# Power-of-two scales made by ScalarE, and the first row roots on ScalarE, in a fused H3 convolution and SiLU feed-forward kernel

## The chip, the cores and the metric

The kernel runs on one core of a Trainium2 chip. The metric is device time in microseconds of one execution; the median of three runs of the kernel before is 1259.5 us. The core's engines work side by side, each with its own queue of instructions in a fixed order: TensorE (PE, matmuls into PSUM banks), VectorE (DVE, elementwise), ScalarE (ACT, activations with a per-partition scale and bias, and an optional sum over the row), GpSimd (POOL) and SyncE (SP), which here issue DMAs. They meet by semaphores only.

## The reference

For x = A_q (2048 rows of 1024), with a layer norm over the columns:

```python
xn = _layernorm(x, axis=-1)                     # (x - mean) / sqrt(var + 1e-5)
# _A_ref: q = xn
k_shift = sum over t of k_pad[:, t:t + S, :] * shift_k[:, ks - 1 - t]
kv = k_shift * v
y = irfft2(rfft2(kv padded) * rfft2(ssm_k padded))[:S] + kv * ssm_D
a = xn * y
# _B_ref
b = silu(xn @ w1) @ w2                          # w1 1024 x 3584, w2 3584 x 1024
out = x + a + b
```

## The kernel before, in words

All large products run on TensorE in float16. Each float32 operand is split into a high half (ScalarE, `split` at L369: copy times a scale) and a low half (VectorE, the difference), and each product is three matmuls: high by high, high by low, low by high (L887 to L889 for the first layer, L1016 to L1018 for the second, L1462 to L1464 and L1653 to L1655 for the convolution's transforms). For the halves to keep their bits, every operand is first brought to a fitting size by a **power of two** taken from its own energy. These scales are what the change is about.

Stages. In the first 80 us the 16 row tiles of x are loaded and normalized (`ln_rows`, L479), the first eight are transposed on TensorE (`turned`, L540) and split, and the first w1 columns are squared, scaled and split (`scales_w1`, L662, `factors_w1`). The first two column pairs of w1 are used plainly (`plain_unit`), over the four upper row tiles and then over the four lower ones; the others go through seven products instead of eight (Strassen's scheme, `units`, with `evacuate` emptying the banks on ScalarE and VectorE). The second layer does the same with the plain part first (`steps2`, `units2`). From about 190 us on the long convolution (`convolution`, from L1291) is woven between those matmuls, in eight groups of 128 channels: gate and short convolution (`gate`), split, forward transform on TensorE and VectorE, product in the frequency domain, `result_scales`, inverse transform, and the gating with xn (`gated`), whose results GpSimd adds to the output in HBM.

The order of all instructions is made before the program runs. Every piece of work is an `Op` with an engine, an estimated duration and the tiles that it reads and writes; generators yield Ops, and the planner `Order.run` (L176) takes at each step the Op that could start first by its own estimates, minus the generator's bias. So a changed Op in one place can move any later instruction of the program. The planner also adds 1.28 us where an Op needs another ScalarE table than the last one (L192).

The lines that the change touches:

- `norm` (L438): a matmul with ones (L448) sums squares over the partitions into PSUM. One VectorE Op, `chain` (L451), then reduces (L454), takes the maximum with 1e-30 and cuts the number to a power of two by two shifts of its bits (`pow2`, L434 and L435), and calls `then`.
- `then` in `scales_w1` (L680 to L682): two products with constants and a reciprocal, for the five scales of a column pair. In `gate` (L1384): a reciprocal and two products, for the signal and filter scales. In `result_scales` (L1564): four instructions, the last two multiplying by scales of the signal.
- `ln_rows`: statistics of each row tile (L497, L499), then for a group of row tiles (2, 2, 4 and 8 tiles) a chain of eleven VectorE instructions (L506 to L516): the inverse root by a first guess from the bits and two corrections. Then the rows are normalized, tiles 4 to 7 by ScalarE (L526), the others by VectorE (L528).
- `a_act` (L354): an activation; only Silu was marked as needing a table.
- The first activation (L1725) loads ScalarE's table, that of Silu, which also serves all the copies and squares.

Of the kernel before, what the change touches and what calls it, by code (L numbers as in the profile page):

```python
# [43 lines left out]
LB = 0.15  # L44
ON_ACT = (4, 5)
APPLY = (4, 5, 6, 7)
GUESS = 0x5f3759df

PRODUCTS = {"P1": ("A11", "B11"), "P7": ("S3", "T3"), "P6": ("S2", "T2"), "P2": ("A12", "B21"),
# [67 lines left out]
class Order:  # L117
# [4 lines left out]
    def __init__(self):  # L122
        self.free = defaultdict(float)
        self.wrote, self.read = {}, {}
        self.slots, self.patterns = {}, {}
        self.streams = []
        self.pipe = self.now = 0.0
        self.table = AF.Silu

    def cells(self, a):  # L130

# [168 lines left out]
def h3_ffn_kernel(ctx, tc, x, kp, vs, fs, shift, dskip, w1, w2, cfwd, cinv, out):  # L300
# [29 lines left out]
    def T(f, o, ins, us, m=0.1):  # L330
        return Op("PE", us, 0.3, f, ins, [o], m)
# [22 lines left out]
    def a_act(o, i, func, scale=1.0, bias=None, total=None):  # L354
        def f():
            kw = {} if bias is None else {"bias": bias}
            if total is not None:
                kw["accum_out"] = total
            nc.scalar.activation(o, i, func, scale=scale, **kw)  # L359
        ins = [i] + [s for s in (scale, bias) if s is not None and not isinstance(s, float)]  # L360
        p = A(f, o, ins)
        p.table = func if func == AF.Silu else None
        p.busy += 0.07 * (len(ins) - 1) - 0.06 * (i.space == bass.MemoryType.PSUM)
        if total is not None:
            p.busy += 0.19
            p.writes.append(total)
        return p
# [26 lines left out]
    for n, e in enumerate((14 - 64, 10 - 64, 8 - 64, 64 - 23, 64)):  # L394
        nc.vector.memset(powers[:, n:n + 1], 2.0 ** e)
    invc = cst.tile([P, 1], F32, name="invc")
    one = cst.tile([P, 1], F32, name="one")
    nc.vector.memset(one, 1.0)
    ones = one.to_broadcast([P, P])
# [38 lines left out]
    def norm(ring, ss, ns, then, flags, margin=1.5):  # L438

        yield ring.ready  # L440
        pt, tok = ring.tile([P, W])
        yield pw.ready
        e, etok = pw.tile([P, 2])

        cols, n = len(ns), sum(ns)

        def mm():
            nc.tensor.matmul(pt[:, 0:n], ones, ss, start=True, stop=True)  # L448

        def chain():  # L450
            for c, m in enumerate(ns):  # L451
                q = sum(ns[:c])
                if m > 1:
                    nc.vector.tensor_reduce(e[:, c:c + 1], pt[:, q:q + m], axis=AX.X, op=ADD)  # L454
                else:
                    nc.vector.tensor_copy(e[:, c:c + 1], pt[:, q:q + 1])
            pow2(e[:, 0:cols], e[:, 0:cols])
            then(e[:, 0:cols])

        yield T(mm, pt[:, 0:n], [ss], 0.25, m=margin)  # L460
        p = V(chain, e, [pt[:, 0:n]], us=1.1)
        p.writes = p.writes + flags[0]
        yield p
        tok.set()
        etok.set()
        for t in flags[1]:
            t.set()


# [9 lines left out]
    def ln_rows():  # L479
        for t0, n, bias in ((0, 2, 0.26), (2, 2, 0.17), (4, 4, LB), (8, 8, 0.03)):  # L480
            yield bias
            ag = lnp.tile([P, 8, 2], F32, name="ag", bufs=2)
            nt = lnp.tile([P, 3, 8], F32, name="nt", bufs=2)
            order_in = (8, 9, 12, 13, 10, 11, 14, 15) if n == 8 else range(t0, t0 + n)
            for t in order_in:
                yield flag["xt", t]
                xt = xts[t][0]
                if t in ON_ACT:
                    k = t - t0
                    yield a_act(wide, xt, AF.Copy, total=nt[:, 0, k:k + 1])  # L490
                    yield a_act(ag[:, k, 0:1], nt[:, 0, k:k + 1], AF.Copy, 1.0 / D)
                    yield a_act(wide, xt, AF.Square, -1.0, ag[:, k, 0:1], total=nt[:, 0, k:k + 1])
                    yield a_act(ag[:, k, 1:2], nt[:, 0, k:k + 1], AF.Copy, 1.0 / D)
                    continue
                st = lnp.tile([P, 2, 6], F32, name="st", bufs=2)
                for a in range(2):
                    yield V(lambda: nc.vector.bn_stats(st[:, a, :], xt[:, a * W:(a + 1) * W]), st[:, a, :],  # L497
                            [xt[:, a * W:(a + 1) * W]], us=0.65)
                yield V(lambda: nc.vector.bn_aggr(ag[:, t - t0], st), ag[:, t - t0], [st], us=0.2)  # L499
            q = slice(t0, t0 + n)  # L500
            mean, var, r = ag[:, 0:n, 0], ag[:, 0:n, 1], rstd[:, q]
            e, f, v = (nt[:, k, 0:n] for k in range(3))

            def chain():
                tt, ts, stt = nc.vector.tensor_tensor, nc.vector.tensor_scalar, nc.vector.scalar_tensor_tensor
                ts(v, var, EPS, None, op0=ADD)  # L506
# [9 lines left out]
                stt(r, e, 1.5, r, op0=ADD, op1=MUL)  # L516
            p = V(chain, r, [ag[:, 0:n]], us=1.8)
            p.writes += [e, f, v]
            yield p
            for k, t in enumerate(order_in):  # L520
                xt = xts[t][0]
                if k == (0 if t in APPLY else 1):
                    yield V(lambda: nc.vector.scalar_tensor_tensor(nmr[:, q], mean, -1.0, r, op0=MUL, op1=MUL), nmr[:, q], [ag[:, 0:n], r], us=0.2)
# [4 lines left out]
                yield V(lambda: nc.vector.tensor_scalar(xt, xt, ag[:, t - t0, 0:1], rstd[:, t:t + 1], op0=SUB, op1=MUL),  # L528
                        xt, [xt, ag[:, t - t0], rstd[:, t:t + 1]], us=0.78)
                flag["xn", t].set()  # L530
# [131 lines left out]
    def scales_w1():  # L662
        for n, (_, i) in enumerate(pairs):
            yield (0.25, 0.16, 0.1, 0.05)[min(n, 3)]
            m = 4 if n < 2 else 2
            if n >= NP:
                for a in range(m):
                    yield flag["raw", n, a]
                flag["scaled", n].set()
                continue  # L670
            yield sq_r.ready
            ss, tok = sq_r.tile([P, 4])
            for a in range(m):
                yield flag["raw", n, a]
                r = raws[n][2][a]
                yield a_act(junk[:, 0:r.shape[1]], r, AF.Square, total=ss[:, a:a + 1])

            def then(e, i=i):
                sc = wsc[:, i]
                nc.vector.tensor_scalar(sc[:, 3:5], powers[:, 3:5], e, None, op0=MUL)  # L680
                nc.vector.reciprocal(e, e)
                nc.vector.tensor_scalar(sc[:, 0:3], powers[:, 0:3], e, None, op0=MUL)  # L682
            yield from norm(ctxs["nm"], ss[:, 0:m], (m,), then, ([wsc[:, i]], [flag["scaled", n], tok]))

    spills = []

# [604 lines left out]
    def convolution(floor):  # L1291
# [57 lines left out]
        def gate():  # L1349

            for g in range(NG):
# [32 lines left out]
                def then(e):  # L1384
                    nc.vector.reciprocal(sc[:, 0:2], e)
                    nc.vector.tensor_scalar(sc[:, 0:2], sc[:, 0:2], 2.0 ** (15 - 64), None, op0=MUL)
                    nc.vector.tensor_scalar(sc[:, 2:4], e, 2.0 ** 64, None, op0=MUL)
                yield from norm(py_r, ss[:, 0:6], (4, 2), then, ([sc[:, 0:4]], [flag["scales", g]]), 4.0)

        CB = 0.03  # L1390

# [167 lines left out]
        def result_scales(g):  # L1559
# [1 line left out]
            yield flag["energy", g]  # L1561
            sc, ss = scs[g][0], sss[g][0]

            def then(e):  # L1564
                nc.vector.reciprocal(sc[:, 4:5], e)
                nc.vector.tensor_scalar(sc[:, 4:5], sc[:, 4:5], 2.0 ** (15 - 64 - 50), None, op0=MUL)
                nc.vector.scalar_tensor_tensor(sc[:, 5:6], e, 2.0 ** (64 - 41), sc[:, 2:3], op0=MUL, op1=MUL)
                nc.vector.tensor_tensor(sc[:, 5:6], sc[:, 5:6], sc[:, 3:4], op=MUL)
            yield from norm(py_r, ss[:, 8:12], (4,), then, ([sc[:, 4:6]], [flag["un", g], sss[g][1]]), 3.0)

        def inverse(g):

# [149 lines left out]
        yield from load_factors()  # L1722

    warm = lnp.tile([P, 1], F32, name="warm")
    nc.scalar.activation(warm, ones[:, 0:1], AF.Silu)  # L1725
    add(begin(), 0.05)
    add(warm_up(), 0.0)
    add(x_rows(), 0.13)
# [53 lines left out]
```

## Time and profile before

| | us |
|---|---|
| median of three runs (1259.02 to 1259.97) | 1259.5 |
| the profiled execution | 1259.29 |
| its span, first to last instruction | 1257.5 |
| TensorE busy | 1234.0 |
| VectorE busy | 1137.8 |
| ScalarE busy | 724.8 |
| GpSimd busy | 132.8 |

The profile is one execution. A row of a timeline has the start and the duration in us, the engine, the line, the operation, the tile written and the tile read, the shapes and a count; in brackets, how long the engine was idle before it and what ended that. A row of groups has the line, the engine, the operation and the count, then the busy time in us and the mean of one in ns, then the idle time before. Matmuls are pipelined: a 512-column one lasts 0.38 us in its row, but they start 0.21 to 0.22 us apart. Most helpers are one line for many uses (L359 is every activation, L348 and L351 are elementwise VectorE work), so the tile names tell what a row is: `ft` transposes, `ff` banks of the layers, `wo` split factors, `hf` hidden activations, `ht` their split halves, `pow` and `wsc` scales, `spec` and `tmp` the transforms.

### The profile page before, as it was taken

The page shows a single profiled execution, that of the slowest core. Times are in us where ns is not written, and L with a number is a line of the kernel's source. Part 1 is how long each engine was busy: PE and PEld are TensorE (multiplying, and loading weights), DVE is VectorE, ACT ScalarE, POOL GpSimd, SP SyncE. Part 2 cuts the span into 40 slices and gives each one's busy share as a digit, 9 for nine tenths or more (in the row PEclk, how much of TensorE's full clock was granted, in tenths as well). Part 3 has the DMA queues.
Part 4 walks back from the last instruction along what each step waited for, and adds up shares of the span by engine and source line. Part 5 has one row for each costly group of instructions (what it writes and reads, how often), then busy time and mean ns, then how long its engine had stood idle before and what let it go on. Part 6 is the DMA issues. An engine that isn't in the chain of part 4 may idle for free. (4 is left out here: it accounts for less than half of the span.)

```text
span 1257.5 us, 17095 instructions
## 1 busy us (share of the span) xinstructions
PE 1234.0 (98%) x6066; PEld 600.4 (48%) x6066; DVE 1137.8 (90%) x1503; ACT 724.8 (58%) x1148; POOL 132.8 (11%) x141
## 2 busy tenths in 40 slices
PE   7999999999999999999999999999999999999997
PEld 6654444444444544444444544544544444454453
DVE  8999997997999979998999899899989989998961
ACT  7758887776677878568643632643453345552331
POOL 0000000000000110002000300300120120122241
PEclk8999999999999999999999999999999999999999
DMA  9097899889798899679997876789596498988784
GB/s 335 9 332 250 291 312 313 270 264 205 226 386 294 243 306 315 209 195 288 346 315 219 180 200 136 168 257 259 112 238 158 116 204 227 251 140 154 160 143 74
DMA packets 268309, 286.12 MB, mean 228 GB/s; under 512 B 65344, under 2 KB 184128, under 8 KB 266944
## 3 DMA queue, kind: packets, MB, share of 16 engines
q1 hardware_dynamic: 241488, 260.12, 66.8%
q0 software_dynamic: 26736, 24.92, 15.4%
q8 instruction: 47, 0.77, 0.3%
q14 instruction: 38, 0.31, 0.1%
HBM read 184.05 MB, written 96.73 MB: 223 GB/s over the span
## 5 line engine op out<-in xcount | busy, mean ns | idle before, releaser
L1016 PE MATMUL ff<-x,wo 128*128 128x512 f16 x864 | 327.4, 379 | 1.0 <-ACT hf L359 1.0
L1018 PE MATMUL ff<-x,wo 128*128 128x512 f16 x864 | 327.4, 379 | 0.0
L1017 PE MATMUL ff<-x,wo 128*128 128x512 f16 x864 | 327.4, 379 | 0.0
L887 PE MATMUL ff<-x,wo 128*128 128x512 f16 (+1 forms) x808 | 303.5, 376 | 3.9 <-ACT hf L359 2.6
L888 PE MATMUL ff<-x,wo 128*128 128x512 f16 (+1 forms) x808 | 303.5, 376 | 1.4 <-DVE x L351 1.4
L889 PE MATMUL ff<-x,wo 128*128 128x512 f16 (+1 forms) x808 | 303.5, 376 | 0.2 <-DVE wo L351 0.2
L348 DVE TENSOR_TENSOR spec<-spec 128x512 f32<-128x512 f32 (+2 forms) x256 | 261.5, 1052 | 2.4 <-DVE spec L348 0.5
L1018 PEld LDWEIGHTS <-wo 128*128 128x128 f16 x864 | 84.5, 98 | 102.0
L1016 PEld LDWEIGHTS <-wo 128*128 128x128 f16 x864 | 85.5, 99 | 98.8
L1017 PEld LDWEIGHTS <-wo 128*128 128x128 f16 x864 | 84.5, 98 | 100.5 <-issue 1.9
L889 PEld LDWEIGHTS <-wo 128*128 128x128 f16 x808 | 79.2, 98 | 94.6 <-issue 1.7
L888 PEld LDWEIGHTS <-wo 128*128 128x128 f16 x808 | 79.3, 98 | 92.1 <-issue 5.6
L887 PEld LDWEIGHTS <-wo 128*128 128x128 f16 x808 | 80.8, 100 | 86.9
L359 ACT ACTIVATE hf<-ff,invc 128x512 f32<-128x512 f32 x64 | 43.5, 679 | 114.1 <-PE ff L1018 106.5
L345 POOL DMA_DIRECT2D out<-hf x63 | 55.5, 881 | 495.4 <-ACT hf L359 426.6
L348 DVE TENSOR_TENSOR tmp<-spec 128x2048 f32<-128x2048 f32 (+1 forms) x48 | 92.3, 1930 | 0.7
L351 DVE SCALAR_TENSOR_TENSOR ht<-hf,wsc,ht 128x1024 f16<-128x1024 f32 (+1 forms) x56 | 67.2, 1201 | 7.3 <-ACT ht L359 7.2
L345 POOL DMA_DIRECT2D out<-xg x40 | 44.9, 1333 | 262.8 <-DVE hf L348 108.4
L359 ACT ACTIVATE spec<-ps 128x512 f32<-128x512 f32 x84 | 48.7, 591 | 36.8 <-PE ps L1464 35.9
L359 ACT ACTIVATE wo<-raw,wsc 128x512 f16<-128x512 f32 (+1 forms) x56 | 51.6, 927 | 27.6 <-DVE raw L348 14.8
L359 ACT ACTIVATE spec<-spec 128x1024 bf16<-128x1024 f32 x32 | 33.7, 1054 | 57.4 <-DVE spec L348 57.1
L351 DVE SCALAR_TENSOR_TENSOR acc<-kin,taps,acc 128x1024 f32<-128x1024 f32 x48 | 61.3, 1277 | 2.2 <-ACT acc L359 2.2
(171 smaller groups left out, 1769.6 us busy)
## 6 DMA issues: line engine op xcount, KB each, us to landing
wo<-hs SPq DMA_DIRECT2D x160, 256.0 KB, 4.0
hs<-ht SPq DMA_DIRECT2D x80, 256.0 KB, 5.2
out<-hf POOLq DMA_DIRECT2D x63, 256.0 KB, 4.4
raw<-in_w SPq DMA_DIRECT2D x28, 512.0 KB, 6.0
wraw<-in_w SPq DMA_DIRECT2D x24, 512.0 KB, 6.1
w2n<-in_w SPq DMA_DIRECT2D x24, 512.0 KB, 6.6
kin<-in_kp SPq DMA_DIRECT2D x16, 704.0 KB, 6.0
xt<-in_x SPq DMA_DIRECT2D x16, 512.0 KB, 7.5
```

Of the source, the lines that this page charges most:

```text
L345: return Op("POOL", 1.1, 3.0, lambda: nc.gpsimd.dma_start(o, i, accum_op=ADD), [i], [o], m, 2.3 * n)
L348: return V(lambda: nc.vector.tensor_tensor(o, a, b, op=op), o, [a, b], **k)
L351: return V(lambda: nc.vector.scalar_tensor_tensor(o, a, s, b, op0=op0, op1=op1), o, [a, b] + ([] if isinstance(s, float) else [s]), **k)
L359: nc.scalar.activation(o, i, func, scale=scale, **kw)
L887: nc.tensor.matmul(o, w[:, 0, k], xf[:, :, k, 0], start=first and k == 0, stop=False, **kw)
L888: nc.tensor.matmul(o, w[:, 0, k], xf[:, :, k, 1], start=False, stop=False, **kw)
L889: nc.tensor.matmul(o, w[:, 1, k], xf[:, :, k, 0], start=False, stop=last and k == KH - 1, **kw)
L1016: nc.tensor.matmul(po, hx[:, n, 0, :], wc[:, n, 0, :], start=first and n == 0, stop=False, **kw)
L1017: nc.tensor.matmul(po, hx[:, n, 0, :], wc[:, n, 1, :], start=False, stop=False, **kw)
L1018: nc.tensor.matmul(po, hx[:, n, 1, :], wc[:, n, 0, :], start=False, stop=last and n == 3, **kw)
```

## The change

1. A new `norm_on_two` takes the place of `norm` for 28 chains: the 12 column pairs of w1 from the third on, and the signal and result scales of each of the eight groups. The sum over the columns is taken by ScalarE (Identity with a tiny bias 2^-100 in place of the maximum, and the row sum), one per column of the result. VectorE then does two instructions, both shifts in one and the reciprocal. The scales themselves are made by one-column activations on ScalarE (`small`), two or three for each chain.
2. The first four row tiles (two groups) take sqrt(var + eps) on ScalarE and a reciprocal on VectorE, in place of the eleven instructions.
3. The first table is that of Sqrt; a table load for Silu comes ahead of the first silu.

```diff
+ROOTED = 4
-        self.table = AF.Silu
+        self.table = AF.Sqrt
-        p.table = func if func == AF.Silu else None
+        p.table = func if func in (AF.Silu, AF.Sqrt) else None
+    def small(o, i, scale, ins=()):
+        return Op("ACT", 0.2, 0.2, lambda: nc.scalar.activation(o, i, AF.Copy, scale=scale), [i, *ins], [o], 0.15)
+
+    def norm_on_two(ring, ss, ns, then, flags, margin=1.5):
...
+        def halved():
+            a, r = e[:, 0:cols], e[:, 2:2 + cols]
+            nc.vector.tensor_scalar(a.bitcast(I32), a.bitcast(I32), 24, 23,
+                                    op0=ALU.logical_shift_right, op1=ALU.logical_shift_left)
+            nc.vector.reciprocal(r, a)
+
+        yield T(mm, pt[:, 0:n], [ss], 0.25, m=margin)
+        for c, m in enumerate(ns):
+            q = sum(ns[:c])
+            p = a_act(e[:, 8:8 + m], pt[:, q:q + m], AF.Identity, 1.0, tiny, total=e[:, c:c + 1])
+            p.busy = 0.4
+            yield p
+        tok.set()
+        yield V(halved, e[:, 0:4], [e[:, 0:2]], us=0.34)
+        yield from then(e[:, 0:cols], e[:, 2:2 + cols])
...
-            p = V(chain, r, [ag[:, 0:n]], us=1.8)
-            p.writes += [e, f, v]
-            yield p
+            if t0 < ROOTED:
+                p = a_act(v, var, AF.Sqrt, 1.0, eps)
+                p.busy = 0.2
+                yield p
+                yield V(lambda: nc.vector.reciprocal(r, v), r, [v], us=0.18)
+            else:
+                p = V(chain, r, [ag[:, 0:n]], us=1.8)
+                p.writes += [e, f, v]
+                yield p
...
+            if n < 2:
+                yield from norm(ctxs["nm"], ss[:, 0:m], (m,), then, ([wsc[:, i]], [flag["scaled", n], tok]))
+                continue
+
+            def scales(e, r, i=i):
+                sc = wsc[:, i]
+                yield small(sc[:, 3:5], powers[:, 3:5], e, [e])
+                yield small(sc[:, 0:3], powers[:, 0:3], r, [r])
+            yield from norm_on_two(ctxs["nm"], ss[:, 0:m], (m,), scales, [flag["scaled", n], tok])
...
+                def scales(e, r):
+                    yield small(sc[:, 0:2], r, 2.0 ** (15 - 64))
+                    yield small(sc[:, 2:4], e, 2.0 ** 64)
+                    yield small(sc[:, 6:7], sc[:, 2:3], sc[:, 3:4], [sc[:, 3:4]])
+                yield from norm_on_two(py_r, ss[:, 0:6], (4, 2), scales, [flag["scales", g]], 4.0)
...
+            def scales(e, r):
+                yield small(sc[:, 4:5], r, 2.0 ** (15 - 64 - 50))
+                yield small(sc[:, 7:8], e, 2.0 ** (64 - 41))
+                yield small(sc[:, 5:6], sc[:, 7:8], sc[:, 6:7], [sc[:, 6:7]])
+            yield from norm_on_two(py_r, ss[:, 8:12], (4,), scales, [flag["un", g], sss[g][1]], 3.0)
...
-    nc.scalar.activation(warm, ones[:, 0:1], AF.Silu)
+    nc.scalar.activation(warm, ones[:, 0:1], AF.Sqrt)
```

The matmuls, their number and their data stay as they were.

More of the change, by code (lines that the diff above doesn't have):

```diff
@@ L396, in h3_ffn_kernel @@
     invc = cst.tile([P, 1], F32, name="invc")
+    tiny = cst.tile([P, 1], F32, name="tiny")
+    nc.vector.memset(tiny, 2.0 ** -100)
+    eps = cst.tile([P, 1], F32, name="eps")
+    nc.vector.memset(eps, EPS)
     one = cst.tile([P, 1], F32, name="one")
@@ L442, in norm @@
         yield pw.ready
-        e, etok = pw.tile([P, 2])
+        e, etok = pw.tile([P, 16])
         cols, n = len(ns), sum(ns)
@@ L466, in norm, with mm @@
         for t in flags[1]:
+            t.set()
+    def small(o, i, scale, ins=()):
+        return Op("ACT", 0.2, 0.2, lambda: nc.scalar.activation(o, i, AF.Copy, scale=scale), [i, *ins], [o], 0.15)
+    def norm_on_two(ring, ss, ns, then, flags, margin=1.5):
+        yield ring.ready
+        pt, tok = ring.tile([P, W])
+        yield pw.ready
+        e, etok = pw.tile([P, 16])
+        cols, n = len(ns), sum(ns)
+        def mm():
+            nc.tensor.matmul(pt[:, 0:n], ones, ss, start=True, stop=True)
+        def halved():
[12 more added lines that the diff above has]
+        yield from then(e[:, 0:cols], e[:, 2:2 + cols])
+        etok.set()
+        for t in flags:
             t.set()
@@ L682, in then @@
                 nc.vector.tensor_scalar(sc[:, 0:3], powers[:, 0:3], e, None, op0=MUL)
-            yield from norm(ctxs["nm"], ss[:, 0:m], (m,), then, ([wsc[:, i]], [flag["scaled", n], tok]))
+            if n < 2:
[6 more added lines that the diff above has]
+            yield from norm_on_two(ctxs["nm"], ss[:, 0:m], (m,), scales, [flag["scaled", n], tok])
     spills = []
@@ L1382, in gate @@
                         tok.set()
[L1384 to L1388, printed above, removed]
+                def scales(e, r):
[3 more added lines that the diff above has]
+                yield from norm_on_two(py_r, ss[:, 0:6], (4, 2), scales, [flag["scales", g]], 4.0)
         CB = 0.03
@@ L1562, in result_scales @@
             sc, ss = scs[g][0], sss[g][0]
[L1564 to L1569, printed above, removed]
+            def scales(e, r):
[3 more added lines that the diff above has]
+            yield from norm_on_two(py_r, ss[:, 8:12], (4,), scales, [flag["un", g], sss[g][1]], 3.0)
         def inverse(g):
```

## The prediction

> **What bounds the kernel now.** First the busy shares and the stretches of the run, because they say how much any change of this kind can bring at all.
>
> ```profile
> PE 1234.0 (98%) x6066; PEld 600.4 (48%) x6066; DVE 1137.8 (90%) x1503; ACT 724.8 (58%) x1148; POOL 132.8 (11%) x141
> ```
>
> ```profile
> 0.00:60.00 60.00, 50.74 (x326) 36.72 (x327) 53.41 (x138) 43.50 (x81) 0.69 (x6) 0.94 0.50 180
> 60.00:240.00 180.00, 179.56 (x863) 85.11 (x862) 166.52 (x272) 137.66 (x192) 0.95 (x1) 1.00 0.87 291
> 240.00:600.00 360.00, 356.54 (x1731) 170.26 (x1730) 334.53 (x418) 267.72 (x416) 20.15 (x19) 1.00 0.90 268
> 600.00:1140.00 540.00, 538.45 (x2624) 256.85 (x2623) 506.05 (x594) 246.68 (x420) 82.31 (x84) 1.00 0.82 206
> 1140.00:1220.00 80.00, 80.00 (x397) 38.77 (x396) 73.61 (x79) 23.18 (x34) 18.79 (x21) 1.00 0.78 155
> 1220.00:1257.50 37.50, 28.67 (x133) 12.73 (x130) 3.69 (x5) 6.08 (x9) 9.92 (x11) 0.96 0.56 77
> ```
>
> In the stretches the columns after the length are the busy time of PE, PEld, DVE, ACT and POOL, the granted clock, and DMA. TensorE is busy for 1234.0 of 1257.5 us. It is idle for 9.3 us in the first 60, for 0.4 + 3.5 + 1.5 = 5.4 us from 60 to 1140, for nothing to 1220, and for 8.8 us in the last stretch. The change alters no matmul, so it can win only out of these 23.5 us. VectorE at 90% looks like the second limit, but its load counts only where TensorE waits for it. So next the waits of TensorE:
>
> ```profile
> PE ft L547 <- DVE x L351: 3.8, 3, 2.1
> PE ft L547 <- DVE xt L528: 2.8, 2, 2.4
> PE ff L887 <- ACT hf L359: 2.6, 3, 1.4
> PE ff L888 <- DVE x L351: 1.4, 2, 1.0
> PE ps L1462 <- ACT tmp L359: 1.2, 2, 0.6
> PE ff L887 <- DVE hf L348: 1.2, 1, 1.2
> ...
> PE ff L1016 <- ACT hf L359: 1.0, 2, 0.8
> ```
>
> The columns are microseconds in total, times, and the longest. Transposes (L547) and the first plain matmuls (L888) wait 3.8 + 2.8 + 1.4 = 8.0 us for VectorE, and these lie in the first stretch, with its 9.3 us of idle. After 60 us TensorE waits almost only for ScalarE's evacuations (L359): 2.6 + 1.2 + 1.0 us, and once 1.2 us for VectorE. So relieving VectorE has something to win at the start. Later it is ScalarE, to which the change gives work, that is late.
>
> **The change, part by part.** *What VectorE loses and ScalarE gains.*
>
> ```profile
> L434 DVE TENSOR_SCALAR pow<-pow 128x1 f32<-128x1 f32 (+1 forms) x31 | 4.9, 158 | 1.1
> ...
> L682 DVE TENSOR_SCALAR wsc<-powers,pow 128x3 f32<-128x3 f32 x14 | 3.2, 229 | 0.5
> ...
> L359 ACT ACTIVATE hf<-ff 128x512 f32<-128x512 f32 x52 | 30.6, 588 | 13.7 <-PE ff L889 13.1
> ...
> L359 ACT ACTIVATION_READ_ACCUMULATOR hi<-kf 128x1 f32 x16 | 3.0, 187 | 0.0
> ...
> L359 ACT ACTIVATE wo<-x,wsc 128x512 f16<-128x512 f32 x8 | 5.7, 715 | 0.1
> ...
> L359 ACT ACTIVATE junk<-xt,ag 128x1024 bf16<-128x1024 f32 x2 | 2.3, 1152 | 0.0
> L359 ACT ACTIVATE junk<-xt 128x1024 bf16<-128x1024 f32 x2 | 2.1, 1049 | 0.0
> ...
> L359 ACT ACTIVATE ag<-nt 128x1 f32<-128x1 f32 x4 | 0.8, 208 | 0.1
> ```
>
> Twenty-eight power-of-two chains change: 12 of w1, 8 of signal scales, 8 of result scales. On VectorE each goes from six or seven instructions of 0.15 to 0.23 us (1.1 to 1.3 us with the gaps) to two of 0.16 (0.35 us): 28 x 0.9 = 25 us. The two rooted row groups lose ten instructions each, 2 x 2.0 us. Together this is 29 of 1137.8 us. On ScalarE each chain adds one or two accumulating activations (0.21 + 0.19 each) and two or three one-column ones. A per-partition operand costs 1152 - 1049 = 103 ns, so a w1 chain adds about 0.4 + 2 x 0.3 = 1.0 us, a signal chain 0.8 + 3 x 0.21 = 1.45, a result chain 1.05. That is 12 + 11.6 + 8.4 = 32 us, plus two roots of 0.3 us and one more table load. ScalarE goes from 58% to 61%. On either engine this is hidden behind the matmuls; if that cover were gone, each chain would cost its 1.0 to 1.5 us.
>
> *The start, walked through in the order in which the changed program stands.*
>
> ```profile
> 7.57 0.17 DVE L506 TENSOR_SCALAR nt<-ag 128x2 f32<-128x2 f32 x1
> ...
> 8.18 0.63 ACT L359 ACTIVATE junk<-x 128x512 bf16<-128x512 f32 x1
> ...
> 9.55 0.16 DVE L516 SCALAR_TENSOR_TENSOR rstd<-nt,rstd 128x2 f32<-128x2 f32 x1
> ...
> 9.75 0.81 DVE L528 TENSOR_SCALAR xt<-xt,ag,rstd 128x1024 f32<-128x1024 f32 x1
> ...
> 11.27 1.28 DVE L497 BATCH_NORM_STATS2 st<-xt 128x6 f32<-128x512 f32 x2
> ...
> 13.63 1.88 DVE L351 SCALAR_TENSOR_TENSOR x<-ft,x 128x512 f16<-128x512 f32 x3
> ...
> 14.46 1.09 PE L547 MATMUL ft<-ident,xt 128*128 128x128 f32 x4 [2.06 <-DVE x L351]
> ...
> 16.22 0.39 PE L889 MATMUL ff<-x,wo 128*128 128x256 f16 x1 [0.25 <-DVE wo L351]
> ...
> 22.34 0.81 DVE L528 TENSOR_SCALAR xt<-xt,ag,rstd 128x1024 f32<-128x1024 f32 x1
> ...
> 33.36 0.38 PE L887 MATMUL ff<-x,wo 128*128 128x512 f16 x1
> ```
>
> Before, the first row chain runs from 7.57 to 9.71 us. In the changed order ScalarE's root stands behind the second w1 square, so it starts at 8.18, where the third square started. With 0.3 us for it and 0.16 for the reciprocal, the subtraction (L528) starts at 8.7 instead of 9.75: 1.0 us earlier, not the 2.0 that the chain loses, since ScalarE is not free at 7.57. The statistics of row tile 2 follow at 10.2 (11.27 before). The changed order then has one low-half split (L351) ahead of w1's chain where before all three stood behind it. The fourth transposes wait for the bank that this split frees, and come at 12.3 instead of 14.46. But the low half of the first w1 factor stands behind the chain, two more splits and half a row tile's statistics. It ends at 15.8, so the third matmul (L889) starts near 15.9 instead of 16.22. Of 2 us won at the transposes 0.3 are left: the next late thing is the w1 factor.
>
> The second root follows w1's four high halves (wo<-x, 0.72 us each, with a split and two squares between them, from 13.6 on) at 18.3. Its rows are subtracted at 19.3 instead of 22.34, and TensorE's waits behind them go. TensorE reaches the first full-width matmul (33.36 before) some 3.4 us earlier. That lead does not last:
>
> ```profile
> 33.36 4.63 ACT L359 ACTIVATE xt<-xt,nmr,rstd 128x1024 f32<-128x1024 f32 x4 [1.26 <-DVE nmr L523]
> ...
> 41.01 1.88 DVE L351 SCALAR_TENSOR_TENSOR x<-ft,x 128x512 f16<-128x512 f32 x3
> ...
> 48.27 1.28 DVE L351 SCALAR_TENSOR_TENSOR x<-ft,x 128x512 f16<-128x512 f32 x2
> ...
> 49.50 0.38 PE L887 MATMUL ff<-x,wo 128*128 128x512 f16 x1
> 49.72 0.38 PE L888 MATMUL ff<-x,wo 128*128 128x512 f16 x1
> ```
>
> ```profile
> 0.74 1.28 ACT L1725 ACT_TABLE_LOAD   x1 [0.74 <-PEq L1772]
> ```
>
> Row tiles 4 to 7 keep the long chain and are normalized by four ScalarE activations (33.36 to 38.0). In the changed order these stand behind both squares of the third w1 pair, the new table load (1.28 us, as the first one took) and the first silu. By the same durations they start at 33.4, where they were. VectorE's splits behind them start at 40.9 (41.01 before). Of the splits that end the lower left block the last but one (48.27 before) starts at 47.6, because a difference of w1 has moved behind it. So the matmul that waits for the whole block (49.50) starts at 48.7: **0.8 us earlier** is what is left of the start. Bounds: nothing, if the four activations slip by 0.8 us; 2.5 us, if the lead of 3.4 us mostly survives.
>
> A row speaks about that table load: 1.28 us, on an engine that had nothing ahead of it. The Trainium skill's page "ScalarE: Activation LUTs", section "What ACT_TABLE_LOAD costs", gives 1283 ns for the load and about 1380 ns of drain, 2.66 us for each switch; the load agrees with the row, and no run here shows the drain with work ahead. By that the start would gain 0.8 - 1.4 = -0.6 us.
>
> *The middle.* The small activations stand in ScalarE's queue, and two or three of them wait for VectorE's new two-instruction step; the evacuation copies stand behind them. A copy (hf<-ff, 0.59 us) has the 12 matmuls of the next product to be done, 12 x 0.22 = 2.6 us by the spacing of the rows at 49.50 and 49.72. From 60 to 240 us ScalarE is busy 76%, with jobs of up to 1.15 us. Bounds: the 5.4 us of idle can go almost entirely, or grow by one wait of up to 1.4 us (the longest for hf above) at each of some ten chains. The whole order behind 60 us is replanned, and which waits arise depends on tenths of a microsecond. I take **nothing** here, between the two.
>
> *The end.* The last writes and the 8 us behind the last matmul keep their order; the convolution's last writes stand further ahead of it, hidden anyway. **Nothing.**
>
> Sum: the profiled execution took 1259.29 us, its span 1257.5 and 1.8 around it, near the median 1259.5. 1259.3 - 0.8 = **1258.5 us**.
>
> **The rivals.**
> *The middle gains* (chance 0.22). VectorE's 29 us less lets ScalarE's queue flow, since many of its jobs wait for VectorE:
>
> ```profile
> ACT hf L359 <- DVE hf L348: 18.9, 12, 7.0
> ...
> ACT wo L359 <- DVE raw L348: 14.8, 10, 4.0
> ```
>
> If half of the middle's idle goes, 2.7 us, and the start gives 0.8 to 1.5: about 1255.5. Against it: TensorE itself waited for VectorE only once there (1.2 us).
>
> *ScalarE late at the evacuations* (0.22), the rival on the slower side. Place: a scale activation at the head of ScalarE's queue waits for VectorE's step, in a stage where VectorE is busy 93% (166.52 of 180), and an evacuation copy is behind it. It decides where ScalarE reaches the copy more than 2.6 - 0.6 = 2.0 us after its product: one 1.15 us job plus a wait of 0.9. Price: waits like those present, 0.9 us in the mean (2.6 us in 3). At six of the 28 chains this is 5 us: 1258.5 + 5 = 1263.5. For it: three waits of this kind exist without the change. Against it: from 60 to 240 us, where ScalarE's load is highest, TensorE idles 0.44 us in all.
>
> *The start gives nothing* (0.14): the table switch or the silu ahead of the four activations costs the 0.8 us or more, 1259.3 to 1260.
>
> **How the numbers follow.** The forecast has 0.42. A measurement of this kernel can tell about 0.2% from no change, 2.5 us: faster is below 1257.0, slower above 1262.0. Faster: the gaining middle, most of it, and a little of the forecast: 0.25. Slower: most of the evacuation rival and unlucky replanning, 0.20. Within: 0.55. The range goes from 1255.0, half of the middle gained and more at the start, to 1262.8, four late evacuations without a gain at the start.
>
> **What would show it.** In the profile after, the first subtraction should start near 8.7 us, the second pair near 19.3, the first full-width matmul near 30 and the matmul of the lower block near 48.7; the second table load should take 1.3 us with a silu right behind. VectorE should be busy some 29 us less, ScalarE some 33 more. TensorE's waits behind 60 us should sum to 4 to 8 us. The prediction is wrong if those waits exceed 10 us with releases by hf evacuations behind a scale activation, if they fall below 3 us, or if more than 2 us of the early lead is still there at 60 us.

## The result and the profile after

The changed kernel took **1267.2 us** (median of five runs, 1265.2 to 1269.4) beside 1259.1 us for the kernel before (five runs, 1257.1 to 1260.0): a ratio of 1.0062, with a 95% interval of 1.0051 to 1.0073. It is 8 us slower. The forecast was 0.8 us faster, and the time lies above the range's upper end of 1262.8.

The profiled execution took 1267.19 us with a span of 1265.4, 7.9 us longer than before. First the page's line of busy times, after the change:

```profile
PE 1237.0 (98%) x6066; PEld 601.3 (48%) x6066; DVE 1116.5 (88%) x1357; ACT 747.9 (59%) x1295; POOL 132.8 (10%) x141
```

VectorE lost 21.3 us and ScalarE gained 23.1 (29 and 33 were forecast), so the work moved as described. TensorE executes the same 6066 matmuls, yet it is busy 3.0 us longer. Its idle time is 1265.4 - 1237.0 = 28.4 us, 4.9 more than before. The two together are the 7.9 us. The stretches of after say where they lie; the columns are those of before (busy PE, PEld, DVE, ACT, POOL, then the granted clock):

```profile
0.00:60.00 60.00, 51.56 (x330) 37.26 (x331) 51.58 (x119) 46.13 (x90) 0.69 (x6) 0.97 0.50 180
60.00:240.00 180.00, 179.73 (x863) 85.17 (x862) 161.38 (x235) 147.04 (x231) 0.95 (x1) 1.00 0.89 297
240.00:600.00 360.00, 353.57 (x1711) 168.61 (x1710) 334.35 (x388) 269.53 (x452) 20.16 (x19) 1.00 0.88 264
600.00:1140.00 540.00, 535.78 (x2604) 255.33 (x2603) 502.87 (x547) 254.97 (x475) 79.59 (x81) 1.00 0.81 204
1140.00:1228.00 88.00, 88.00 (x435) 42.35 (x433) 62.57 (x67) 24.48 (x40) 25.38 (x27) 1.00 0.82 164
1228.00:1265.40 37.40, 28.31 (x131) 12.55 (x129) 3.70 (x5) 5.77 (x9) 6.04 (x7) 0.96 0.43 64
```

Take the length minus PE's busy time in each row. The first 60 us have 8.4 us of idle, 0.8 less than before: the start did win. From 60 to 1140 us the idle grew from 5.4 to 0.27 + 6.43 + 4.22 = 10.9 us, by 5.5, and from 60 to 240, where ScalarE is most loaded, it did not grow at all. The end has 0.3 us more. TensorE's waits after the change (us in total, times, longest):

```profile
PE ff L941 <- ACT hf L360: 4.9, 3, 2.4
PE ft L593 <- DVE x L352: 3.3, 3, 1.3
PE ff L941 <- DVE hf L349: 1.8, 1, 1.8
PE ps L1516 <- ACT tmp L360: 1.7, 1, 1.7
...
PE ff L1070 <- ACT hf L360: 0.8, 1, 0.8
```

The transposes' waits for VectorE (L593) fell from 3.8 + 2.8 us to 3.3 and one of 1.2. New are a few long waits of first-layer matmuls (L941, which was L887) for hidden activations: three of together 4.9 us, where it was 2.6 with a longest of 1.4, and one of 1.8 us. Two of the long ones are at 451 and 597 us. The timeline around the first, ScalarE and the matmul that waits:

```profile
442.94 1.35 POOL L346 DMA_DIRECT2D kf<-in_dskip  x1
...
449.06 1.06 ACT L360 ACTIVATE hi<-kf 128x1024 bf16<-128x1024 f32 x1 [4.80 <-DMA kf<-in_dskip]
...
451.16 0.67 ACT L360 ACTIVATE hf<-ff,wsc 128x512 f32<-128x512 f32 x1
451.73 1.13 ACT L360 ACTIVATE acc<-kin,taps 128x1024 f32<-128x1024 f32 x1
...
453.15 0.57 ACT L360 ACTIVATE hf<-ff 128x512 f32<-128x512 f32 x1
...
453.78 0.58 PE L941 MATMUL ff<-x,wo 128*128 128x512 f16 x1 [2.42 <-ACT hf L360]
```

The brackets tell it. GpSimd issues a transfer of 0.5 KB that adds the skip weights to the filter (L1389). ScalarE, whose queue has the filter's squares (hi<-kf) at its head, can go on only 6.1 us after that issue, and stands for 4.80 us. The evacuation copies (hf<-ff) are behind the squares, so TensorE gets its bank 2.4 us late. No scale activation of the change is in this chain. All of these instructions were there before; the planner has put them into another order. It counts at least 1.1 + 3.0 = 4.1 us for such a transfer; in the median the eight take 4.7 us.

The one that ends at 599.8 us looks alike, with other transfers. ScalarE, same kernel:

```profile
593.02 1.15 ACT L360 ACTIVATE x<-wraw,tau 128x1024 f16<-128x1024 f32 x1 [1.52 <-DMA wraw<-in_w]
...
594.92 1.15 ACT L360 ACTIVATE x<-w2n,tau 128x1024 f16<-128x1024 f32 x1 [0.27 <-DMA w2n<-in_w]
...
596.97 1.26 ACT L360 ACTIVATE xg<-xg,nmr,rstd 128x128 f32<-128x128 f32 x3 [0.33 <-DMA xg<-in_x]
...
599.18 0.57 ACT L360 ACTIVATE hf<-ff 128x512 f32<-128x512 f32 x1
```

ScalarE loses 1.52 + 0.27 + 0.33 = 2.1 us to loads of weights and rows, has no other gap on the way to the copy that ends the wait, and TensorE waits 2.25 us for that copy. This reading is not tested: no run takes these loads away. Not every wait of the middle is of this kind: the one of 1.7 us for tmp, up to 684.04 us, comes after ScalarE has stood 6.28 us for VectorE's work on the transform.

Last the 3.0 us for which TensorE is busier. Stretches around both waits, same columns:

```profile
451.00:453.70 2.70, 0.35 (x2) 0.08 (x1) 0.80 (x1) 2.70 (x7) 0.00 (x0) 0.97 1.04 381
453.70:456.70 3.00, 2.92 (x7) 0.99 (x7) 3.00 (x4) 2.22 (x6) 0.00 (x0) 0.50 0.97 347
...
597.40:599.80 2.40, 0.16 (x1) 0.00 (x0) 2.35 (x4) 2.40 (x6) 0.00 (x0) 1.00 0.89 291
599.80:603.30 3.50, 3.49 (x10) 1.34 (x10) 3.35 (x4) 2.64 (x3) 0.00 (x0) 0.57 0.97 289
```

Behind the waits the granted clock (the number after POOL's) is 0.50 for 3.0 us and 0.57 for 3.5 us. Seven matmuls are done where there is time for fourteen at 0.216 us, and ten where there is time for sixteen. By the clock that is 3.0 x 0.50 + 3.5 x 0.43 = 3.0 us, the whole of TensorE's added busy time. So these two waits cost 2.42 and 2.25 us of idle, and each about 1.5 us of half clock behind it.

The sum: start -0.8, middle +5.5, half clock +3.0, end +0.3: 8.0 us, against 7.9 measured.

### The profile page after: what moved, and what is told of

Its sections match the earlier page's. It is cut to its first block, busy times and chain, and to the rows that moved or that the text cites. A ratio compares the mean times of both kernels' runs of the same rounds, so it can differ in the third digit from the quotient of the medians.

```text
span 1265.4 us, 17090 instructions
## 1 busy us (share of the span) xinstructions
PE 1237.0 (98%) x6066; PEld 601.3 (48%) x6066; DVE 1116.5 (88%) x1357; ACT 747.9 (59%) x1295; POOL 132.8 (10%) x141
## 4 chain that ended last, share of the span: by engine, by line
PE 63%; DVE 6%; DMA 6%; issue 3%; ACT 2%; SPq 0%; POOL 0%; POOLq 0%; ACTq 0%; DVEq 0%
PE ff L1070 11%; PE ff L1071 11%; PE ff L1072 11%; PE ff L941 7%; PE ff L943 7%; PE ff L942 7%; DVE spec L349 2%; DMA w2n<-in_w 2%; PE ps L1516 2%; PE ps L1518 2%; PE ps L1517 2%; DVE x L352 1%; DMA out<-in_x 1%; DMA xg<-in_x 1%; PE py L1708 1%
## 5 line engine op out<-in xcount | busy, mean ns | idle before, releaser
L941 PE MATMUL ff<-x,wo 128*128 128x512 f16 (+1 forms) x808 | 305.0, 377 | 8.4 <-ACT hf L360 4.9
L941 PEld LDWEIGHTS <-wo 128*128 128x128 f16 x808 | 81.0, 100 | 89.5 <-ACT wo L360 1.9
L346 POOL DMA_DIRECT2D out<-xg x42 | 47.9, 1311 | 256.3 <-DMA hsfS<-ht 111.7
L360 ACT ACTIVATE ht<-hf,wsc 128x1024 f16<-128x1024 f32 (+1 forms) x56 | 60.7, 1084 | 3.9 <-DVE hf L349 1.7
L352 DVE SCALAR_TENSOR_TENSOR wo<-raw,wsc,wo 128x512 f16<-128x512 f32 (+1 forms) x56 | 56.4, 1011 | 5.8 <-ACT wo L360 5.8
```

The source lines that it names most:

```text
L346: return Op("POOL", 1.1, 3.0, lambda: nc.gpsimd.dma_start(o, i, accum_op=ADD), [i], [o], m, 2.3 * n)
L352: return V(lambda: nc.vector.scalar_tensor_tensor(o, a, s, b, op0=op0, op1=op1), o, [a, b] + ([] if isinstance(s, float) else [s]), **k)
L941: nc.tensor.matmul(o, w[:, 0, k], xf[:, :, k, 0], start=first and k == 0, stop=False, **kw)
```

## The experiments

The theory after reading the traces: **the planner's new order costs the time, the moved work does not**. The rivals: ScalarE's added activations delay the evacuations (the prediction's own slower rival), and the one transfer of skip weights explains it all. A ratio is always to the kernel before on the same chip, with its 95% interval.

### Order and work apart: e1 and e2

`e1` keeps the changed kernel's order on the queues of TensorE and SyncE, but VectorE does the added ScalarE work at the same places:

```diff
-        return Op("ACT", 0.2, 0.2, lambda: nc.scalar.activation(o, i, AF.Copy, scale=scale), [i, *ins], [o], 0.15)
+        return Op("ACT", 0.2, 0.2, lambda: nc.vector.tensor_scalar(o, i, scale, None, op0=MUL), [i, *ins], [o], 0.15)
...
+            p.emit = lambda c=c, q=q, m=m: nc.vector.tensor_reduce(e[:, c:c + 1], pt[:, q:q + m], axis=AX.X, op=ADD)
...
+                p.emit = chain
...
-    nc.scalar.activation(warm, ones[:, 0:1], AF.Sqrt)
+    nc.scalar.activation(warm, ones[:, 0:1], AF.Silu)
```

> The changed kernel's plan is kept instruction for instruction on TensorE and SyncE; every activation that the change added is done by VectorE at the same place of the order (the sums over columns, the one-column scales, the long root chain of the first two row groups), and Silu's table is the only one. Theory A (the replanned order makes the waits): the middle waits stay, 1265 to 1269 us, less nothing. Theory B (the added work on ScalarE makes the evacuations late): the waits of the middle that stand behind ScalarE go, 1258 to 1261 us.

`e2` is the other half: the order of before, with the 28 chains and two roots done as in the change, inside the old Ops, so that the planner sees nothing of it:

```diff
+            if scales is not None:
+                for c, m in enumerate(ns):
+                    q = sum(ns[:c])
+                    nc.scalar.activation(e[:, 8:8 + m], pt[:, q:q + m], AF.Identity, scale=1.0, bias=tiny, accum_out=e[:, c:c + 1])
+                a, r = e[:, 0:cols], e[:, 2:2 + cols]
+                nc.vector.tensor_scalar(a.bitcast(I32), a.bitcast(I32), 24, 23,
+                                        op0=ALU.logical_shift_right, op1=ALU.logical_shift_left)
+                nc.vector.reciprocal(r, a)
+                scales(a, r)
+                return
...
+                if t0 < 4:
+                    nc.scalar.activation(v, var, AF.Sqrt, scale=1.0, bias=eps)
+                    nc.vector.reciprocal(r, v)
+                    return
```

> The plan of the kernel before is kept instruction for instruction on TensorE and SyncE; the sums, scales and the first two roots are done as the changed kernel does them, ScalarE's share standing in its queue where VectorE's chain stood in the emission. Theory A (order): 1257 to 1261 us, as before. Theory B (work): 1264 to 1268 us, with new waits of TensorE behind ScalarE at the chains.

Measured: `e1` 1268.5 us, ratio 1.0076 (1.0061 to 1.0091); `e2` 1258.2 us, ratio 0.9995 (0.9984 to 1.0005). In the traces TensorE's matmuls of `e1` come in the sequence of after and those of `e2` in the sequence of before, but for a few rows that are missing. This is a table of two by two, in us:

| | scales and roots on VectorE | on ScalarE |
|---|---|---|
| order of before | 1259.1 | 1258.2 |
| order of after | 1268.5 | 1267.2 |

Read down a column, the order costs 9 us whoever does the work. Read along a row, moving the work changes about 1 us, which for the order of before can't be told from nothing. The page lines show that the work really moved, `e2` first:

```profile
PE 1233.1 (98%) x6066; PEld 600.0 (48%) x6066; DVE 1118.1 (89%) x1357; ACT 751.4 (60%) x1295; POOL 132.8 (11%) x141
```

```profile
PE 1237.2 (98%) x6066; PEld 601.1 (47%) x6066; DVE 1129.3 (89%) x1485; ACT 724.0 (57%) x1148; POOL 132.9 (10%) x141
```

`e2` has ScalarE at 751.4 us, more than after itself, and TensorE's busy time is not raised; `e1` has ScalarE at 724.0, as before, and yet TensorE at 1237.2 us: the half clock is there (0.55 from 603 to 606 us) without any of the change's ScalarE work. The middle stretches of `e2`:

```profile
240.00:600.00 360.00, 356.67 (x1732) 170.13 (x1731) 330.83 (x386) 274.09 (x453) 20.13 (x19) 1.00 0.90 268
600.00:1140.00 540.00, 540.00 (x2636) 257.67 (x2634) 500.89 (x546) 257.49 (x478) 82.33 (x84) 1.00 0.82 206
```

and of `e1`:

```profile
240.00:600.00 360.00, 355.88 (x1727) 169.89 (x1726) 339.25 (x420) 266.99 (x421) 20.13 (x19) 1.00 0.89 267
600.00:1140.00 540.00, 534.17 (x2589) 254.15 (x2587) 504.69 (x589) 244.16 (x413) 79.66 (x81) 0.99 0.81 203
```

The idle is 3.3 + 0.0 us in `e2` and 4.1 + 5.8 in `e1`. (The profiled execution of `e2` is the fastest of its ten, 1256.0 us.)

ScalarE does stand at the head of its queue for the new work. In after, the sums wait for TensorE's matmul with ones, and the scales for VectorE's step:

```profile
ACT pow L360 <- PE py L488: 16.7, 9, 3.7
...
ACT csc L477 <- DVE pow L494: 13.7, 8, 3.1
```

In `e2` the same two waits come to 16.8 us (10 times) and 16.2 us (16 times, the longest 3.0), and TensorE's idle time in the middle is no greater than before. So the small activations delay no evacuation that matters; the rival of the late ScalarE falls.

### The one wait at 451 us: e3

`e3` leaves the skip weights' transfer out, and so the skip term of the convolution, with all else in the order of after:

```diff
-                        yield G(kf[0:1, 0, 0, :], dskip[g:g + 1, :])
+                        p = G(kf[0:1, 0, 0, :], dskip[g:g + 1, :])
+                        p.emit = lambda: None
+                        yield p
```

> The changed kernel in its own order, but the small accumulating DMA of the skip weights (dskip into kf) is not issued, so the skip term is left out; ScalarE no longer waits for it ahead of the squares of kf. If the wait at 451 us (2.6 us, and seven matmuls at half clock behind it, 1.5 us) is that DMA's: about 4 us less, 1263 us. If ScalarE would be late there anyway: 1266 to 1268 us.

Measured: 1262.3 us, ratio 1.0027 (1.0014 to 1.0039), by the ratios 4.4 us less than after. The stretch around 451 us, first in after, then in `e3`, then in `e1`:

```profile
440.00:460.00 20.00, 17.58 (x75) 7.54 (x74) 15.30 (x13) 12.95 (x23) 1.94 (x2) 0.91 1.05 323
```

```profile
440.00:460.00 20.00, 20.00 (x94) 9.10 (x93) 18.19 (x17) 16.38 (x29) 1.11 (x1) 1.00 1.10 351
```

```profile
440.00:460.00 20.00, 20.00 (x93) 9.01 (x92) 15.99 (x15) 16.55 (x28) 1.94 (x2) 1.00 1.13 358
```

After does 75 matmuls in these 20 us, `e3` 94, at full clock and without idle. So the transfer is the cause of this wait and of the half clock behind it, 19 x 0.216 = 4.1 us. It isn't the whole loss: a ratio of 1.0027 stays, and from 60 to 1140 us `e3` still idles 9.1 us, only 1.8 less than after. What it has back is most of all the clock: TensorE is busy 1233.4 us, 3.6 less than in after, and the half clock at 600 us is gone too, though the nearest transfer that was left out stood at 565 us. And `e1`, with the same order and with the transfer, has no wait here either; it does 93 matmuls in the stretch and loses its time elsewhere, in the last of its rows above and in waits like these:

```profile
PE ff L943 <- DVE hf L349: 4.1, 3, 2.1
...
PE ps L1518 <- ACT tmp L360: 2.3, 1, 2.3
PE ff L943 <- ACT hf L360: 1.9, 1, 1.9
```

The same transfer is as slow in `e1` (6.3 us from its issue at 441.87), but ScalarE reaches the squares 4.3 us after the issue and stands only 2.0 us; in after it is there 1.3 us after the issue. So the same order of queues can have other waits when two engines are 3 us further apart or closer together, and a single wait is not the explanation, only one item of it.

### How much a new order alone moves: n2, n5, n3, n4

If the order is the cause, then changing nothing but an estimate in the planner, with the same instructions, must move the time by several us too. `n2` and `n5` do it to the kernel before, `n3` and `n4` to the changed one:

```diff
-        p = V(chain, e, [pt[:, 0:n]], us=1.1)
+        p = V(chain, e, [pt[:, 0:n]], us=0.95)
```

```diff
-        p = V(chain, e, [pt[:, 0:n]], us=1.1)
+        p = V(chain, e, [pt[:, 0:n]], us=1.05)
```

```diff
-        return Op("ACT", 0.2, 0.2, lambda: nc.scalar.activation(o, i, AF.Copy, scale=scale), [i, *ins], [o], 0.15)
+        return Op("ACT", 0.3, 0.2, lambda: nc.scalar.activation(o, i, AF.Copy, scale=scale), [i, *ins], [o], 0.15)
```

```diff
-        yield V(halved, e[:, 0:4], [e[:, 0:2]], us=0.34)
+        yield V(halved, e[:, 0:4], [e[:, 0:2]], us=0.44)
```

> The kernel before with the same instructions, only the planner's estimate of the scale chain is 0.95 us and not 1.1, so that the order is planned anew. Theory A (the order alone moves the time by several us): it differs from 1259 us by 2 us or more, either way. Theory B: within 1257 to 1261 us, since no work has moved.

> The kernel before, planned with 1.05 us for the scale chain in place of 1.1. Theory A: a draw again, 1257 to 1268, so that the plan of before (1259) is one of the better draws if it lies above. Theory C: 1257 to 1262.

> The changed kernel with the same instructions, planned anew because the planner's estimate of a one-column activation is 0.3 us and not 0.2. Theory A (each plan is a draw, several us apart): anywhere from 1256 to 1270, off from 1267 by 2 us or more. Theory C (the changed work always gives a bad plan, through its estimates): 1265 to 1269.

> The same with the estimate of VectorE's two-instruction step 0.44 us and not 0.34. Theory A: 1256 to 1270, off from both 1267 and the last one. Theory C: 1265 to 1269.

Measured: `n2` 1264.0 (1.0039, 1.0024 to 1.0054), `n5` 1261.3 (1.0016, 1.0007 to 1.0026), `n3` 1272.0 (1.0101, 1.0084 to 1.0118), `n4` 1265.9 (1.0050, 1.0035 to 1.0065). An estimate changed by a twentieth of a microsecond costs the kernel before 2 us, and one changed by 0.15 us costs 5. For the changed kernel 0.1 us in one estimate costs 5 us more (`n3`), and in another it gives 1 us that the intervals can't tell from nothing (`n4`). So `n2` and `n3` bear the theory out, `n3` even above the range given for a draw (1256 to 1270); `n4` and `n5` lie as well in the ranges that were set for the other answer, that the changed work itself always leads the planner to a bad order. The middle stretches of `n2` show more idle, as in after (4.4 + 3.6 us), but no fallen clock:

```profile
240.00:600.00 360.00, 355.58 (x1727) 169.75 (x1726) 340.16 (x420) 268.41 (x423) 20.07 (x19) 1.00 0.90 267
600.00:1140.00 540.00, 536.41 (x2614) 255.69 (x2614) 510.23 (x597) 243.68 (x411) 81.42 (x83) 1.00 0.81 203
```

### The roots alone: e4

`e4` is the kernel before with the roots on ScalarE and the tables, planned anew; the 28 chains stay on VectorE:

```diff
+            if t0 < ROOTED:
+                p = a_act(v, var, AF.Sqrt, 1.0, eps)
+                p.busy = 0.2
+                yield p
+                yield V(lambda: nc.vector.reciprocal(r, v), r, [v], us=0.18)
+            else:
+                p = V(chain, r, [ag[:, 0:n]], us=1.8)
...
-    nc.scalar.activation(warm, ones[:, 0:1], AF.Silu)
+    nc.scalar.activation(warm, ones[:, 0:1], AF.Sqrt)
```

> The kernel before with only the first four rows' roots on ScalarE (and the tables for it), planned anew. By the prediction's walk the start gains 0.8 us; the middle is a draw. Theory A: 1257 to 1268 with waits of the middle that none of the roots' instructions stand near. If the middle were tied to the scale chains (theory B or C): 1257 to 1260.

Measured: 1266.4 us, 1.0049 (1.0030 to 1.0068). Most of the loss of the whole change, with nothing of the chains in it. In its profile TensorE idles 8.6 us from 60 to 1140 us, and 11.7 us behind that, where it was 8.8 before. So a small change at the start is enough to set off the replanning.

### Better orders for the changed kernel: v1 to v4

If single waits come from wrong estimates, better ones should help. `v1` tells the planner 6.0 us for the landing of the skip weights, `v2` gives the evacuations a greater bias (0.2 for 0.06), `v3` gives that bias to the kernel before, and `v4` does both to the changed one:

```diff
+                        p.late = 6.0
```

```diff
-    EB = 0.06
+    EB = 0.2
```

> The changed kernel, planned with the landing of the skip weights' DMA 6.0 us after its issue slot instead of 3.0, near the 5 to 6 us that the profiles show; instructions the same, order anew. If a wrong landing estimate is what spoils this plan: the wait at 451 us goes and nothing takes its place, 1261 to 1264 us. Theory A (a draw of the plan): anywhere from 1257 to 1272, with other waits.

> The changed kernel, planned with the preference of the feed-forward evacuations raised from 0.06 to 0.2 us; instructions the same. If the evacuations are late because the planner lets other ScalarE jobs in front of them: the waits near 325, 597 and 1094 us shrink, 1258 to 1263 us. Theory A: a draw, 1257 to 1272.

> The kernel before with the same raised preference. If it is a lever and no draw: below 1259, 1254 to 1258 us. Theory A: 1257 to 1270, no better than the other replans of before.

> The changed kernel with both, the landing of 6.0 us and the preference of 0.2. If both are levers: 1255 to 1260 us. Theory A: a draw, 1257 to 1272, not the sum of the two.

Measured: `v1` 1259.3 (1.0001, 0.9988 to 1.0013), `v2` 1259.4 (1.0000, 0.9988 to 1.0013), `v3` 1270.9 (1.0091, 1.0063 to 1.0119), `v4` 1264.4 (1.0038, 1.0024 to 1.0052). Either step alone brings the changed kernel back to the time of before, but the two together give 5 us of it away again, and the second makes the kernel before 12 us slower. `v1` did what it was told: ScalarE stands 2.3 us in all for the skip weights, where it was 15.8 in after. But in the kernel before it stands 9.2 us for them without harm, and in `v4`, with the same estimate, 2.8. `v1` came out better than its single cause allowed for (1261 to 1264), `v2` in the range of either answer, `v3` above both, and `v4` only in that of a draw. A draw was given 1257 to 1272 (1270 for `v3`), so wide that these runs could hardly speak against it. So neither step is shown to be a remedy; that each is another draw fits, and is not proven. No version was measurably faster than the kernel before. All kernels in one table, by TensorE's idle time from 60 to 1140 us in the profiled execution (length less busy time). The span is all idle time plus the busy time; the median is that of all executions, and the profiled one of `v4` is the fastest of its ten:

| kernel | idle 60 to 1140, us | all idle, us | TensorE busy, us | span, us | median, us |
|---|---|---|---|---|---|
| `e2` order of before, work on ScalarE | 3.3 | 21.2 | 1233.1 | 1254.3 | 1258.2 |
| `v2` | 4.6 | 23.4 | 1233.4 | 1256.8 | 1259.4 |
| before | 5.4 | 23.5 | 1234.0 | 1257.5 | 1259.1 |
| `v1` | 6.2 | 23.6 | 1232.5 | 1256.1 | 1259.3 |
| `v4` | 6.5 | 25.5 | 1234.5 | 1260.0 | 1264.4 |
| `n5` | 6.9 | 25.0 | 1234.7 | 1259.7 | 1261.3 |
| `n2` | 8.0 | 27.4 | 1233.0 | 1260.4 | 1264.0 |
| `e4` | 8.6 | 29.0 | 1237.0 | 1266.0 | 1266.4 |
| `e3` without the skip term | 9.1 | 26.1 | 1233.4 | 1259.5 | 1262.3 |
| `v3` | 9.7 | 32.0 | 1235.4 | 1267.4 | 1270.9 |
| `e1` order of after, work on VectorE | 10.0 | 29.3 | 1237.2 | 1266.5 | 1268.5 |
| `n4` | 10.7 | 28.8 | 1236.2 | 1265.0 | 1265.9 |
| after | 10.9 | 28.4 | 1237.0 | 1265.4 | 1267.2 |
| `n3` | 13.0 | 31.4 | 1238.6 | 1270.0 | 1272.0 |

The kernel before's instructions in four orders (before, `n5`, `n2`, `v3`) take 1259 to 1271, in the mean 1263.8; the changed ones in six (after, `n3`, `n4`, `v1`, `v2`, `v4`) take 1259 to 1272, in the mean 1264.7. These are few draws, and `v1` to `v4` were aimed. The kernel before is the best of its four, the changed kernel the second slowest of its six, so luck of the draw can be part of the 8 us. It is not shown to be all of it. Without the aimed ones, the three orders of the kernel before take 1259 to 1264 us, and the three of the changed kernel 1266 to 1272, as does `e4` with 1266. That the changed Ops lead the planner to worse orders more often than not is a rival that these runs leave open. It need not be so each time, since `v1` and `v2` take 1259.

## Why the prediction was wrong, point by point

**The start: right.** The rows of after, in time order:

```profile
8.57 0.28 ACT L360 ACTIVATE nt<-ag,eps 128x2 f32<-128x2 f32 x1
...
9.08 0.81 DVE L574 TENSOR_SCALAR xt<-xt,ag,rstd 128x1024 f32<-128x1024 f32 x1
...
19.55 0.81 DVE L574 TENSOR_SCALAR xt<-xt,ag,rstd 128x1024 f32<-128x1024 f32 x1
...
30.97 0.19 ACT L360 ACTIVATION_READ_ACCUMULATOR junk<-raw 128x1 f32 x1
31.18 1.28 ACT L360 ACT_TABLE_LOAD   x1
32.47 0.69 ACT L360 ACTIVATE hf<-ff,wsc 128x512 f32<-128x512 f32 x1
33.06 1.23 ACT L360 ACTIVATE xt<-xt,nmr,rstd 128x1024 f32<-128x1024 f32 x1
...
48.28 0.38 PE L941 MATMUL ff<-x,wo 128*128 128x512 f16 x1
```

The first subtraction is at 9.08 (8.7 forecast), the second pair at 19.55 (19.3), the four activations from 33.06 (33.4), the matmul of the lower block at 48.28 (48.7; before 49.50). The first was late because the second square waited 0.64 us for its load. So 1.2 us were won at that matmul, where 0.8 were forecast, and the term has the right sign and size. `e1`, with the order of after and the long root chain, idles 10.3 us in the first 60, against 8.4. The rival of the table switch falls: the silu starts 1.29 us after the load does. The Trainium skill, "ScalarE: Activation LUTs", section "What ACT_TABLE_LOAD costs", has 1283 ns for the load, which agrees, and about 1380 ns of drain, of which these rows show nothing, though ScalarE had worked up to the load (30.97 + 0.19 us).

**The work moved: right within a third.** VectorE lost 21.3 us (29 forecast), ScalarE gained 23.1 (33 forecast), and both were hidden, as `e2` shows.

**The middle: the step that failed.** "The whole order behind 60 us is replanned, and which waits arise depends on tenths of a microsecond. I take **nothing** here, between the two." The words name the cause and the number doesn't follow from them. The middle cost 5.5 us of idle and 3.0 us of half clock. Two things were missed. The orders measured show that new orders of the same instructions spread over 12 us, and the kernel before is the best of its four. So by these few the value to expect of a new draw was not zero but some us slower: 2 and 5 us in the two where only an estimate was changed. And the bound on one wait, "up to 1.4 us", came from the longest wait of the old order; the new ones go up to 2.4 us in after and 5.2 in `n3`, and some bring the half clock, for which the sum had no term at all. The range was also narrower than the prediction's own bounds for this step: ten waits of 1.4 us are 14 us, but its upper end allowed for four of 0.9.

**The slower rival: right in sign, wrong in cause.** "ScalarE late at the evacuations" gave 1263.5, half of the loss, and the two longest waits are indeed evacuations behind ScalarE's queue. But the jobs at its head waited for transfers (4.80 us for skip weights; 1.52 us for a weight block), not for VectorE's step, and `e1` is as slow without a single scale activation. The test that the prediction set for it, releases by hf evacuations "behind a scale activation", was not met, while its bound of 10 us for the waits behind 60 us was exceeded.

**The gaining middle: refuted as a net effect.** In the order of before, `e2` has 3.3 us of idle in the middle, 2.1 less, in its fastest execution; the ratio of 0.9995 doesn't tell that from nothing.

What stays open: why the order of before is better than most, and whether the changed Ops draw from worse orders. The runs show a spread of 12 us, not which property of an order makes it good.

## What to carry to other kernels

Where a planner orders the whole program and one engine is 98% busy, a changed Op is two changes, the work and a new order: keep the order and change only the work (as in `e2`) to price the first, and change one estimate without touching the work (as in `n2`) to see the spread of the second. Here the order of before was the best of its four, and a local saving of 1 us came with a loss of several when everything behind it was planned anew. A single wait that explains half of a loss (`e3`) is still no explanation of why the time is worse, if another order with the same work has other waits of the same sum.

## What the runs showed of the hardware

**Half clock after waits of 2.4 us, but not always.** In after, waits of 2.42 and 2.25 us were each followed by some 3 us at a granted clock of 0.50 to 0.57, 1.5 us lost each time. In `n2` two longer waits, 2.92 us up to 329.70 and 2.55 up to 601.74, were not:

```profile
326.50:329.60 3.10, 0.29 (x2) 0.01 (x1) 3.10 (x5) 2.32 (x3) 0.72 (x1) 1.00 0.37 148
329.70:332.70 3.00, 3.00 (x14) 1.36 (x14) 3.00 (x4) 1.22 (x2) 0.00 (x0) 1.00 0.83 235
599.00:601.70 2.70, 0.19 (x1) 0.00 (x0) 2.70 (x4) 2.28 (x4) 0.00 (x0) 1.00 0.88 276
601.80:604.80 3.00, 3.00 (x15) 1.34 (x15) 3.00 (x3) 0.40 (x1) 0.00 (x0) 1.00 1.04 247
```

The clock stays at 1.00 and 14 and 15 matmuls are done in 3 us. So the length of the wait alone doesn't decide. Nor, it seems, does the order: this profiled execution of `n2` has a mean granted clock of 0.998 and took 1262.2 us; its three others have 0.992 to 0.994 and took 1263.2 to 1266.1. In `v4` the profiled one has 0.995 and 1261.8 us, the nine others 0.990 to 0.993 and 1263.3 to 1266.8. Only the profiled executions have a trace, so where the clock fell in the others, and what decides it, these runs don't show. The Trainium skill, "TensorE: Matmul & The Clock Gate", section "HAM oscillation — how this bites in real kernels", gives as its rule no idle gaps over about 3.4 us; here the half clock followed gaps of 2.42 and 2.25 us.

**Small accumulating transfers land late and unevenly.** The row of DMA issues of after (count, size, median us from issue to landing):

```profile
kf<-in_dskip POOLq DMA_DIRECT2D x8, 0.5 KB, 4.7
```

The eight transfers took 3.1 to 6.2 us, 4.7 in the median, from issue to landing; the one issued at 442.94 us was among the slowest.
